# Soft-MoE after attention: the bias and maximum rows of the score matmuls held in bfloat16, with single buffers for two scratch tiles and more weights fetched in attention

## The chip, the cores and the metric

The kernel runs on one NeuronCore of one Trainium2 chip. The metric is the device time of one execution in microseconds (us), as the median of several runs. Beside it stands one profiled execution of the kernel before, whose rows are read below: its own time is 441.82 us and its span (first to last instruction) 440.1 us, so 1.7 us lie around the span.

The engines are TensorE (PE; its weight loads are listed as PEld), VectorE (DVE), ScalarE (ACT), GpSimd (POOL) and SyncE (SP), which here does nothing but issue DMAs.

## The reference

Eight batches of causal attention with eight heads (576 positions, head size 64) and a bias made of running sums, and behind them one soft mixture of experts over all 4608 tokens (8 experts of 4 slots, 512 to 1024 to 512). The inputs q and k are the drawn values times 8. Cut to what is computed:

```python
scores = q @ k.T / 8                                   # per head, 576 x 576
cum    = cumsum(max(s, 0))
bias   = -(cum[:, None] - cum[None, :])
scores = where(causal, -1e9, scores + min(bias, 0))
attn   = exp(scores - max(scores)); attn /= attn.sum() + 1e-9
x      = (attn @ v) as 4608 rows of 512
logits = x @ phi                                       # 32 slots
d      = softmax(logits over the tokens)               # dispatch
h      = relu((d.T @ x)[expert] @ w1[expert]); slot_out = h @ w2[expert]
out    = softmax(logits over the slots) @ slot_out
```

## The kernel before

**The work.** The 64 heads are taken as 32 pairs p, four pairs to a batch; the two heads of a pair use the two halves of TensorE's rows. For each pair the program makes these steps (their names are those of the planner):

- load and load_v bring q, k and v; cast and low split q and k into a high and a low part in a tile w (float32r).
- A tile g carries what is added to the scores through a matmul of its own. Its rows hold ones, the parts of the running sums (step cum, a DMA, L293) and the parts of the row maxima (step md, a DMA, L359). Three such tiles turn over.
- mx (L311) computes approximate scores with the high parts, and adds the sums with a second matmul whose weights are the tile ones2. red (L323) lets DVE add the mask and take the maximum of each row: twelve instructions with accumulator for a pair, each followed by a short read of the accumulator. Their full-size output goes to a scratch tile, junk, and is never read; junk has two buffers.
- f0 (POOL, L338 and L339) splits the maxima in two parts, f1 (PE, L346) transposes them, f2 (ACT) copies them out of PSUM, and md writes them into g.
- s (L377) computes the scores from four matmuls per block: three of w's parts, and the last with g, which adds the bias and takes the maximum away. ex (ACT, L388) takes the exponential, cut (POOL, L395) zeroes what lies above the diagonal.
- zc and z (POOL, L421 to L427) add up the columns, ax and a (PE, L467 and L478; rows named x and y) multiply with v, ev (ACT, L490) copies the result out of PSUM, and sm (L507) sums rows with a tile of unit columns, onesl.

For each batch, e1 (L595) takes the reciprocals of the sums, rw (L600) writes them to DRAM (rows rs<-sr) and rd (L517) reads them back broadcast (rows arena<-rs); nr (L540) multiplies. nat transposes the result, lt (L619, L623) computes the logits, c0 to c1 copy and transpose them, and t2 to t8 keep a running maximum (nmin, L733), running totals (tot) and running slot inputs (acc, L779). For the last pair the reciprocals come through a matmul instead (rb), and nr is L537.

**The combine weights.** Eight more chains, one per batch, turn the softmax over slots into operands for the last stage: sp (L698 on DVE, L700 on ACT, L702 on DVE) writes three parts of a batch's values to a tile en, ct (PE, L709, rows ctb and cta) transposes them, and cd (L717 and L718, DVE for even batches and ACT for odd ones) copies them out of PSUM. ct of any batch waits for all of s. en has two buffers, so sp of batch b waits for ct of batch b-2. Their result is not used before the last stage.

**After attention.** m0 to m7 finish the slot softmax (pt at L824, i4s at L830). sit (L941) scales acc by i4s; mlp1 (L954), relu, mlp2 (L988), pick (L997) and the combining matmul (L1020) follow, and 18 transfers of 512 KB write the output (L1028).

**The weights.** w1 and w2 are fetched as 64 quarters of 512 KB. NPRE of them (21) go to a tile of their own, pre, during attention. As attention's buffers come free another 22 follow: 17 pieces of the arena, the two halves of one w tile (ww), and the three g tiles (wg, through the helper `slot`). The remaining 21 wait until the first quarters have been used.

**What sets the order.** A planner, `schedule` (L34), orders all steps on the five engines by list scheduling: it knows for each step an estimated time, the steps it comes after, and an urgency from the table PR (L21). PE's queue, and each other engine's, then runs in that order whatever the real times are. Where the planner sees PE idle ahead of the first a step or after the last, `busy` matmuls (L914) fill the gap.

## Time and profile before

| | before |
|---|---|
| median of 3 runs | 446.05 us (444.98 to 446.85) |
| profiled execution | 441.82 us |
| its span | 440.1 us |
| mean granted TensorE clock | 0.978 of full speed |
| busy: PE, PEld, DVE, ACT, POOL | 406.3, 302.5, 309.6, 245.4, 281.4 us |
| DMA | 83.21 MB, mean 189 GB/s |

The rows shown below come from views of that one execution. A row of a timeline gives the start in us, the duration in us, the engine, the line of the kernel, the operation, output<-input, its shape and count, and in brackets the idle time of the engine ahead of it with what ended that wait. In the chain of waits a row gives the start, the duration and the work that held up the end at that time. A row of windows gives a stretch, its length, for each engine its busy time and instructions, the granted clock, the busy share of the DMA engines and GB/s.

### The profile page before, as it was taken

To read this page: it belongs to the slowest core of one execution; us is meant where nothing else is said; L and a number is where in the kernel's file an instruction comes from. 1 tells how busy PE (TensorE), PEld (TensorE's weight loads), DVE (VectorE), ACT (ScalarE), POOL (GpSimd) and SP (SyncE) were. 2 spreads that over 40 slices of the span, in tenths; PEclk is the share of its full clock that TensorE was granted. 3 is DMA by queue.
4 is the path that set the end of the run, shared out by engine and by line. 5 is a ranking of instruction groups with operands and counts; after the bars stand their busy time and mean duration, and the time that the engine had idled before them with its cause. 6 is when DMAs were issued, how large, how long until landed. Compare 5 with 4: busy or idle time off the path is not lost.

```text
span 440.1 us, 14686 instructions
## 1 busy us (share of the span) xinstructions
PE 406.3 (92%) x5625; PEld 302.5 (69%) x5625; DVE 309.6 (70%) x1055; ACT 245.4 (56%) x732; POOL 281.4 (64%) x385
## 2 busy tenths in 40 slices
PE   7999999989999999999999999999999999898960
PEld 6787777777677767766877687777776857344550
DVE  6777767987887888779877887788778486121460
ACT  3146676576658665856675676567665745011350
POOL 7349889878877895888588858887887710000000
PEclk9599999999999999999999999999999999999995
DMA  5317565626664475448544822362247389999988
GB/s 175 108 57 236 157 174 155 212 87 189 193 180 131 137 217 157 131 136 225 152 132 136 231 90 84 105 178 82 87 114 216 95 291 337 392 402 409 384 297 293
DMA packets 54549, 83.21 MB, mean 189 GB/s; under 512 B 5456, under 2 KB 41808, under 8 KB 54480
## 3 DMA queue, kind: packets, MB, share of 16 engines
q1 hardware_dynamic: 54480, 82.29, 59.6%
q8 instruction: 44, 0.72, 0.7%
q14 instruction: 25, 0.20, 0.1%
HBM read 71.84 MB, written 10.06 MB: 186 GB/s over the span
## 4 chain that ended last, share of the span: by engine, by line
PE 66%; DMA 12%; DVE 9%; issue 5%; SPq 3%; POOL 2%; ACT 1%; DVEq 0%
PE s L377 19%; PE y L478 15%; PE mx L311 10%; DMA arena<-rs 7%; PE m L954 3%; DMA rs<-sr 3%; PE m L988 3%; PE sum L507 3%; SPq L517 2%; DVE nmin L733 2%; PE busy L914 2%; PE lt L619 2%; PE nat L548 2%; PE po L1020 2%; DVE junk L323 1%
## 5 line engine op out<-in xcount | busy, mean ns | idle before, releaser
L323 DVE CUSTOM_DVE_ANT_0 junk<-mx,mask 128x448 bf16<-128x448 f32 (+3 forms) x320 | 125.5, 427 | 50.8 <-PE mx L311 25.1
L388 ACT ACTIVATE arena<-s 128x288 f32<-128x288 f32 (+4 forms) x384 | 114.3, 409 | 30.0 <-PE s L377 29.3
L377 PE MATMUL s<-w 64*128 64x288 f32 (+4 forms) x1152 | 109.2, 304 | 0.0
L478 PE MATMUL y<-arena 128*64 128x512 f32 (+4 forms) x640 | 90.1, 427 | 0.0
L377 PEld LDWEIGHTS s<-w 64*128 64x128 f32 (+1 forms) x1152 | 81.7, 177 | 10.1 <-ACT arena L388 1.2
L395 POOL TENSOR_SCALAR_AFFINE_SELECT arena<-arena 128x256 f32<-128x256 f32 (+1 forms) x160 | 69.0, 444 | 23.7 <-ACT arena L388 21.7
L478 PEld LDWEIGHTS y<-arena 128*64 128x64 f32 x640 | 43.0, 137 | 46.4 <-issue 35.8
L421 POOL TENSOR_TENSOR arena<-arena 128x896 f32<-128x896 f32 x31 | 66.4, 2141 | 7.5 <-PE mt L346 5.2
L311 PE MATMUL mx<-w 64*128 64x288 f32 (+4 forms) x384 | 59.3, 314 | 3.7 <-DVE e_nat L664 2.7
L311 PE MATMUL mx<-g,ones 64*128 64x288 f32 (+4 forms) x384 | 56.0, 308 | 1.7 <-DVE ones L227 1.7
L377 PE MATMUL s<-g 64*128 64x288 f32 (+4 forms) x384 | 56.5, 291 | 0.0
L423 POOL TENSOR_TENSOR arena<-arena 128x640 f32<-128x640 f32 x31 | 48.0, 1547 | 2.6
L278 ACT CAST w<-arena 128x576 fp32r<-128x576 f32 x64 | 39.8, 675 | 15.0 <-DMA arena<-in_qk_dram 15.0
L283 DVE TENSOR_TENSOR w<-arena,w 128x576 fp32r<-128x576 f32 x64 | 48.0, 776 | 0.0
L311 PEld LDWEIGHTS mx<-w 64*128 64x128 f32 x384 | 41.1, 190 | 8.1 <-PE s L377 3.8
L490 ACT COPY arena<-y 128x512 f32<-128x512 f32 x32 | 18.8, 588 | 47.0 <-PE y L478 47.0
L311 PEld LDWEIGHTS mx<-g,ones 64*128 64x128 f32 x384 | 41.0, 191 | 2.4 <-POOL g L217 1.9
L540 DVE TENSOR_TENSOR arena<-arena 128x576 f32<-128x576 f32 x31 | 34.7, 1128 | 8.7 <-DMA arena<-rs 8.4
L377 PEld LDWEIGHTS s<-g 64*128 64x128 f32 (+1 forms) x384 | 35.1, 177 | 0.7 <-DMA g<-hl 0.2
L338 POOL TENSOR_SCALAR mh<-mx 128x10 fp32r<-128x10 f32 x32 | 21.5, 672 | 20.4 <-DVE mx L323 20.3
L425 POOL TENSOR_TENSOR arena<-arena 128x384 f32<-128x384 f32 x31 | 31.4, 1013 | 2.4
L323 DVE CUSTOM_DVE_ANT_0 junk<-mx,mask,mx 128x288 bf16<-128x288 f32 x64 | 30.6, 516 | 2.2 <-PE mx L311 1.2
(157 smaller groups left out, 565.8 us busy)
## 6 DMA issues: line engine op xcount, KB each, us to landing
pre<-in_w_dram SPq DMA_DIRECT2D x38, 512.0 KB
arena<-in_qk_dram SPq DMA_DIRECT2D x32, 576.0 KB
arena<-in_w_dram SPq DMA_DIRECT2D x18, 512.0 KB
arena<-rs SPq DMA_DIRECT2D x62, 144.0 KB
arena<-in_v_dram SPq DMA_DIRECT2D x32, 256.0 KB
out_dram<-arena SPq DMA_DIRECT2D x11, 512.0 KB
out_dram<-pre SPq DMA_DIRECT2D x7, 512.0 KB
wg<-in_w_dram SPq DMA_DIRECT2D x5, 512.0 KB
```

Source lines behind the costliest of these rows:

```text
L278: nc.scalar.copy(w[:, QO + S * i:QO + S * (i + 1)], st["raw", p][:, i, :])
L283: nc.vector.tensor_tensor(w[:, QO + S * (2 + i):QO + S * (3 + i)], st["raw", p][:, i, :], w[:, QO + S * i:QO + S * (i + 1)].bitcast(F32), ...
L311: nc.tensor.matmul(ps[a][:, d:d + hi - lo], l[r], t[r, KO + lo:KO + hi], start=t is w, stop=t is gt)
L323: nc.vector.tensor_tensor_reduce(out=junk[r, 0:w], in0=ps[r, d:d + w], in1=mask[r, o:o + w], scale=1.0, scalar=m[:, a, 4:5] if i == 1 else ...
L377: nc.tensor.matmul(ps[a][0:n, d:d + hi - lo], t[r, ko + 128 * j:ko + 128 * j + n], t[r, qo + lo:qo + hi], start=x == 0, stop=x == 3)
L388: nc.scalar.activation(st["p", p][0:n, a, o + lo:o + hi], ps[0:n, d:d + hi - lo], AF.Exp, bias=0.0, scale=0.125)
L395: nc.gpsimd.affine_select(d, d, pattern=[[0, 2], [1, n]], compare_op=ALU.is_ge, fill=0.0, base=0, channel_multiplier=-1)
L421: eng.tensor_tensor(z[:, :, 128:576], pt[:, :, 128:576], pt[:, :, 576:1024], op=ALU.add)
L423: eng.tensor_tensor(z[:, :, 256:576], z[:, :, 256:576], pt[:, :, 1024:1344], op=ALU.add)
L425: eng.tensor_tensor(z[:, :, 384:576], z[:, :, 384:576], pt[:, :, 1344:1536], op=ALU.add)
L478: nc.tensor.matmul(y[r, lo - 64:512], vt[:, j, r], st["p", p][:, g, OFF[j] + lo - 128 * j:OFF[j] + 576 - 128 * j], start=(j == 0), stop=(j ...
L540: nc.vector.tensor_tensor(u, u, st.pop(("r", p)), op=ALU.mult)
```

## The change

- The running sums are split into three bfloat16 parts (before: two of float32r), the maxima into two bfloat16 parts. The tiles g, ones2, mask, mh and hl are bfloat16, so the second matmul of mx, the last of s, and the transpose f1 have bfloat16 operands; f1 uses a bfloat16 identity, identb, made at the start.
- onesl is one window of 63 columns instead of 16 tiles of 32; ph is held once instead of four times over.
- junk has one buffer instead of two, and en has one, so sp of batch b waits for ct of batch b-1.
- The g tiles no longer become weight slots. NPRE is 25, so 25 quarters go to pre, 19 to freed room, and 20 wait.
- The table of urgencies PR stays as it is.

The diff, cut to its core:

```diff
-NPRE = 21
+NPRE = 25
...
-    cumhl = reg("x", 0)[0:NH, 0:2 * S].rearrange("p (l x) -> p l x", l=2)
-    nc.vector.tensor_copy(cumhl[:, 0, :].bitcast(F32R), cum)
-    nc.vector.tensor_tensor(cumhl[:, 1, :].bitcast(F32R), cum, cumhl[:, 0, :], op=ALU.subtract)
-    cumd = pd.tile([NH, 2, S], F32, tag="cum", name="cumd", bufs=1)
+    cumhl = reg("x", 0)[0:NH, 0:3 * S // 2].bitcast(BF16).rearrange("p (l x) -> p l x", l=3)
+    for l in range(3):
+        nc.vector.tensor_copy(cumhl[:, l, :], cum)
+        if l < 2:
+            nc.vector.tensor_tensor(cum, cum, cumhl[:, l, :], op=ALU.subtract)
+    cumd = pd.tile([NH, 3, S], BF16, tag="cum", name="cumd", bufs=1)
...
-    onesl = one.tile([128, 4 * HP, 32], F32, name="onesl")
+    onesl = one.tile([128, 63], F32, name="onesl")
     nc.vector.memset(onesl, 0.0)
-    for a in range(4 * HP):
-        nc.vector.memset(onesl[:, a, a:a + 1], 1.0)
+    nc.vector.memset(onesl[:, 31:32], 1.0)
...
-    ph = one.tile([128, HP, 4 * NS], F32, name="ph")
+    ph = one.tile([128, HP, NS], F32, name="ph")
...
-        t = slot("g", [128, PAD + 2 * S], F32R, f"g{i}")
+        t = one.tile([128, PAD + 2 * S], BF16, name=f"g{i}")
...
-            mask = one.tile([128, S], F32, name="mask")
+            mask = one.tile([128, S], BF16, name="mask")
...
-        (nc.vector if i else nc.gpsimd).memset(t.bitcast(F32), 0.0)
+        (nc.vector if i else nc.gpsimd).memset(t, 0.0)
         for a in (0, 64):
-            nc.gpsimd.memset(t[a:a + 4, 0:KO].bitcast(F32), 1.0)
-            nc.gpsimd.memset(t[a:a + 4, KO:].bitcast(F32), -1.0)
+            nc.gpsimd.memset(t[a:a + 5, 0:KO], 1.0)
+            nc.gpsimd.memset(t[a:a + 5, KO:], -1.0)
...
-    ones2 = one.tile([128, 128], F32R, name="ones2")
+    ones2 = one.tile([128, 128], BF16, name="ones2")
...
+    identb = one.tile([128, 128], BF16, name="identb")
+    nc.vector.tensor_copy(identb, ident)
...
-                junk = p2.tile([128, 448], BF16, tag="junk", name="junk")
+                junk = p2.tile([128, 448], BF16, tag="junk", name="junk", bufs=1)
...
-            mh = p2.tile([128, 2, 2, NCH], F32R, tag="mh", name=f"mh{p}")
+            mh = p2.tile([128, 2, 2, NCH], BF16, tag="mh", name=f"mh{p}")
...
-            nc.tensor.transpose(ps[0:4 * NCH, 0:128], mh.rearrange("p a l c -> p (a l c)").bitcast(F32), ident)
+            nc.tensor.transpose(st["mt", p], mh.rearrange("p a l c -> p (a l c)"), identb)
...
-            hl = p2.tile([4 * NCH, 128], F32R, tag="hl", name=f"hl{p}")
+            hl = p2.tile([4 * NCH, 128], BF16, tag="hl", name=f"hl{p}")
...
-                nc.tensor.matmul(st["lt", b][32 * g:32 * g + 32, 64:192], ph[:, hp, 32 * g:32 * g + 32],
+                nc.tensor.matmul(st["lt", b][32 * g:32 * g + 32, 64:192], ph[:, hp, :],
...
-                st["en", b] = p2.tile([128, NCH, 3, NS], F32R, tag="en", name=f"en{b}")
+                st["en", b] = p2.tile([128, NCH, 3, NS], F32R, tag="en", name=f"en{b}", bufs=1)
...
-        war = [("ct", b - 2)] if b > 1 else []
+        war = [("ct", b - 1)] if b else []
...
-    for kind, n in (("g", NG), ("w", NW)):
+    for kind, n in (("w", NW),):
```

Three places show how instructions move. A row gives the line, the operation, output<-input and the shape. Lines after about L190 are two to four higher in the kernel after.

On DVE, at the program's start, the kernel before splits the sums (arena rows after the scan), sets constants and clears two g tiles:

```order
L179 SCALAR_TENSOR_TENSOR arena<-arena 64x576
L182 CAST arena<-arena 64x576
L183 TENSOR_TENSOR arena<-arena 64x576
L189 MEMSET onesl 128x512
L191 MEMSET onesl 128x1 x16
L194 MEMSET dn 64x128
L214 MEMSET g_134 128x1216
L214 MEMSET g_145 128x1216
L225 MEMSET ones_157 128x128
```

The kernel after, at the same place on DVE:

```order
L179 SCALAR_TENSOR_TENSOR arena<-arena 64x576
L183 CAST arena<-arena 64x576
L185 TENSOR_TENSOR arena<-arena 64x576
L183 CAST arena<-arena 64x576
L185 TENSOR_TENSOR arena<-arena 64x576
L183 CAST arena<-arena 64x576
L192 MEMSET onesl 128x63
L193 MEMSET onesl 128x1
L196 MEMSET dn 64x128
L216 MEMSET g_122 128x608
L216 MEMSET g_133 128x608
L227 MEMSET ones_145 128x64
```

Three instructions on 64x576 have come in ahead of the memsets; the memsets of onesl have become two small ones, and those of g have half the elements.

On SP, in the last pairs of the last batch, the kernel before issues weight quarters (in_w) between the reciprocals' way out (rs<-sr) and back (arena<-rs); rs_0 carries the first two pairs, rs_1 pair 30:

```order
L517 DMA arena<-rs_0_6801 64x2x288 x4
L836 DMA wg_6921<-in_w_dram 128x1024
L836 DMA ww_6932<-in_w_dram 128x1024
L600 DMA rs_1_6947<-sr_6934 128x72
L836 DMA arena<-in_w_dram 128x1024 x3
L517 DMA arena<-rs_1_6947 64x2x288 x2
L836 DMA ww_6932<-in_w_dram 128x1024
```

The kernel after, at the same place on SP:

```order
L521 DMA arena<-rs_0_6787 64x2x288 x4
L840 DMA ww_6907<-in_w_dram 128x1024
L604 DMA rs_1_6931<-sr_6918 128x72
L840 DMA ww_6907<-in_w_dram 128x1024
L521 DMA arena<-rs_1_6931 64x2x288 x2
L840 DMA arena<-in_w_dram 128x1024 x15
```

One quarter instead of two stands ahead of rs<-sr, and one instead of three between it and its way back. The four more quarters of pre stand earlier on SP, in pairs 25 to 28.

On PE, between the end of attention and the first matmul of the experts, the kernel before runs as follows (the figure behind a name is the batch; sl is t7, ctb and cta are ct):

```order
L709 MATMUL ctb6_7218<-ident_61,en6_7186 96x128
L709 MATMUL cta6_7217<-ident_61,en6_7186 96x128 x4
L805 MATMUL pn_7226<-one1_74,mrow_7211 128x1
L771 MATMUL sl7_7229<-arena_77,dn_120 32x512 x4
L775 MATMUL sl7_7229<-arena_77,dn_120 32x128 x4
L709 MATMUL ctb7_7244<-ident_61,en7_7224 96x128
L709 MATMUL cta7_7243<-ident_61,en7_7224 96x128 x4
L824 MATMUL pt_7258<-tot_72,cst_sb_60 128x1
L941 MATMUL sit_7278<-i4s_67,acc_68 128x32 x4
```

The kernel after, at the same place on PE:

```order
L713 MATMUL ctb5_7218<-ident_61,en5_7204 96x128
L713 MATMUL cta5_7217<-ident_61,en5_7204 96x128 x4
L828 MATMUL pt_7226<-tot_72,cst_sb_60 128x1
L916 MATMUL busy_7237<-ident_61 128x128 x3
L713 MATMUL ctb6_7242<-ident_61,en6_7230 96x128
L713 MATMUL cta6_7241<-ident_61,en6_7230 96x128 x4
L916 MATMUL busy_7254<-ident_61 128x128 x5
L713 MATMUL ctb7_7261<-ident_61,en7_7250 96x128
L713 MATMUL cta7_7260<-ident_61,en7_7250 96x128 x4
L943 MATMUL sit_7283<-i4s_67,acc_68 128x32 x4
```

The transposes of batches 6 and 7, which stood ahead of pt, now stand between pt and sit, with eight busy matmuls.

On DVE at the same place, the kernel before finishes the parts of en and the copies of ct ahead of acc and tot:

```order
L702 TENSOR_TENSOR en_7224<-e_nat,en_7224 128x5x32
L717 CAST ct_6978<-cta_7217 96x512
L718 CAST ct_6978<-ctb_7218 96x64
L810 COPY fac<-pn 128x1
L779 SCALAR_TENSOR_TENSOR acc<-acc,al_7171,sl_7229 128x512
L819 SCALAR_TENSOR_TENSOR tot<-tot 128x1
L820 TENSOR_TENSOR tot<-tot,fac 128x1
L828 TENSOR_SCALAR tot<-pt 128x1
L829 RECIPROCAL tot<-tot 128x1
L830 TENSOR_SCALAR i4s<-cst_sb,tot,fac 128x32
L943 COPY sit<-sit 128x128
```

The kernel after, on DVE from tot to sit:

```order
L824 TENSOR_TENSOR tot<-tot,fac 128x1
L702 CAST en_7230<-e_nat 128x5x32
L832 TENSOR_SCALAR tot<-pt 128x1
L833 RECIPROCAL tot<-tot 128x1
L834 TENSOR_SCALAR i4s<-cst_sb,tot,fac 128x32
L706 TENSOR_TENSOR en_7230<-e_nat,en_7230 128x5x32
L721 CAST ct_6962<-cta_7241 96x512
L722 CAST ct_6962<-ctb_7242 96x64
L702 CAST en_7250<-e_nat 128x5x32
L706 TENSOR_TENSOR en_7250<-e_nat,en_7250 128x5x32
L945 COPY sit<-sit 128x128
```

The last part of batch 6's en, the copies of its ct and both parts of batch 7's en on DVE have moved behind i4s; between acc and tot there are now the copies of batch 4's ct and parts of batch 5's en.

More of the change, by code (lines that the diff above doesn't have):

```diff
@@ L155, in slot @@
     def slot(kind, shape, dtype, name):
-        return keep.tile(shape, dtype, tag=kind, name=name, bufs=dict(g=NG, w=NW)[kind])
+        return keep.tile(shape, dtype, tag=kind, name=name, bufs=NW)
     def reg(kind, i):
@@ L223, in tile_attn_softmoe @@
         ws.append(t)
-    ones2 = one.tile([128, 128], F32R, name="ones2")
-    nc.vector.memset(ones2.bitcast(F32), 0.0)
+    ones2 = one.tile([128, 128], BF16, name="ones2")
+    nc.vector.memset(ones2, 0.0)
     for a in (0, 64):
-        nc.vector.memset(ones2[a:a + 2].bitcast(F32), 1.0)
+        nc.vector.memset(ones2[a:a + 3], 1.0)
+    identb = one.tile([128, 128], BF16, name="identb")
+    nc.vector.tensor_copy(identb, ident)
     mx = []
@@ L292, in cum @@
             for a in range(2):
-                nc.sync.dma_start(out=gt[64 * a:64 * a + 2, KO:KO + S].bitcast(F32),
+                nc.sync.dma_start(out=gt[64 * a:64 * a + 3, KO:KO + S],
                                   in_=(cumhl if p < HP else cumd)[2 * p + a:2 * p + a + 1, :, :])
@@ L336, in f0 @@
             use("mx", p, 3)
-            mh = p2.tile([128, 2, 2, NCH], F32R, tag="mh", name=f"mh{p}")
+            mh = p2.tile([128, 2, 2, NCH], BF16, tag="mh", name=f"mh{p}")
             nc.gpsimd.tensor_scalar(mh[:, :, 0, :], m, 1.0, None, op0=ALU.mult)
-            nc.gpsimd.tensor_tensor(mh[:, :, 1, :], m, mh[:, :, 0, :].bitcast(F32), op=ALU.subtract)
+            nc.gpsimd.tensor_tensor(mh[:, :, 1, :], m, mh[:, :, 0, :], op=ALU.subtract)
             st["mh", p] = mh
@@ L345, in f1 @@
             ps = bank("mt")
-            nc.tensor.transpose(ps[0:4 * NCH, 0:128], mh.rearrange("p a l c -> p (a l c)").bitcast(F32), ident)
-            st["mt", p] = ps
+            st["mt", p] = ps[0:4 * NCH, 0:64].bitcast(BF16)
+            nc.tensor.transpose(st["mt", p], mh.rearrange("p a l c -> p (a l c)"), identb)
         op(("f1", p), "PE", 110, (t0, "f1"), f1, [("f0", p), dep("md", old(2))], bank=1, ldw=17)
         def f2():
-            hl = p2.tile([4 * NCH, 128], F32R, tag="hl", name=f"hl{p}")
-            nc.scalar.copy(hl, st.pop(("mt", p))[0:4 * NCH, 0:128])
+            hl = p2.tile([4 * NCH, 128], BF16, tag="hl", name=f"hl{p}")
+            nc.scalar.copy(hl, st.pop(("mt", p)))
             st["hl", p] = hl
@@ L358, in md @@
             for a in range(2):
-                nc.sync.dma_start(out=gt[64 * a + 2:64 * a + 4, 0:KO].bitcast(F32).rearrange("l (c q) -> l c q", c=NCH),
-                                  in_=hl[2 * NCH * a:2 * NCH * (a + 1)].bitcast(F32))
+                nc.sync.dma_start(out=gt[64 * a + 3:64 * a + 5, 0:KO].rearrange("l (c q) -> l c q", c=NCH),
+                                  in_=hl[2 * NCH * a:2 * NCH * (a + 1)])
         op(("md", p), "SP", 1300, (t0, "md"), md, [("f2", p)], dma=28)
@@ L506, in sm @@
                         c = S // 2 * f + SQ * i
-                        nc.tensor.matmul(y[o:o + 32, 0:SQ], onesl[:, 4 * hp + i, :], st["z", p][:, g, c:c + SQ],
+                        nc.tensor.matmul(y[o:o + 32, 0:SQ], onesl[:, 31 - 4 * hp - i:63 - 4 * hp - i], st["z", p][:, g, c:c + SQ],
                                          start=first and i == 0, stop=final and i == 3)
@@ L618, in lt @@
             for g in range(4):
-                nc.tensor.matmul(st["lt", b][32 * g:32 * g + 32, 64:192], ph[:, hp, 32 * g:32 * g + 32],
+                nc.tensor.matmul(st["lt", b][32 * g:32 * g + 32, 64:192], ph[:, hp, :],
                                  st["u", p][:, 64 + 128 * g:192 + 128 * g], start=hp == 0, stop=hp == HP - 1)
             for g in range(4):
-                nc.tensor.matmul(st["lt", b][32 * g:32 * g + 32, 0:64], ph[:, hp, 32 * g:32 * g + 32],
+                nc.tensor.matmul(st["lt", b][32 * g:32 * g + 32, 0:64], ph[:, hp, :],
                                  st["u", p][:, 0:64], start=False, stop=hp == HP - 1, skip_group_check=True)
@@ L888, in get @@
                 dst = arena[:, F * i:F * (i + 1)]
-            elif kind == "g":
-                dst = slot("g", [128, F], F32, f"wg{i}")
             else:
@@ L1090, in layout @@
     HP = H // 2
-    phi = np.tile(moe_phi.reshape(HP, 128, -1).transpose(1, 0, 2), (1, 1, 4))
+    phi = moe_phi.reshape(HP, 128, -1).transpose(1, 0, 2)
     arrays = dict(qk=qk, v=vn, s=s.reshape(B * H, S), phi=phi, w1=w1, w2=w2, cst=constants())
```

## The prediction, made before the kernel was run

> **What bounds the kernel now.** I read the page's busy shares first, then the chain of waits, then windows over its stages, and last the timelines at the places that the change touches. The page:
>
> ```profile
> PE 406.3 (92%) x5625; PEld 302.5 (69%) x5625; DVE 309.6 (70%) x1055; ACT 245.4 (56%) x732; POOL 281.4 (64%) x385
> PE 66%; DMA 12%; DVE 9%; issue 5%; SPq 3%; POOL 2%; ACT 1%; DVEq 0%
> ```
>
> PE is busy for 92% of the span, and the chain that ended last runs over PE for 66% of it. Two rows of the chain, the first transpose of nat in two batches, and the windows of a stretch in attention and of the stages behind it:
>
> ```profile
> 207.11 0.66 PE nat L548 x4
> 250.30 0.66 PE nat L548 x4
> ...
> 250.00:330.00 80.00, 78.63 (x1163) 59.88 (x1165) 63.55 (x230) 51.54 (x159) 64.59 (x84) 1.00 0.39 108
> 380.00:400.00 20.00, 19.39 (x216) 8.20 (x212) 3.10 (x5) 2.39 (x4) 0.00 (x0) 1.00 1.02 396
> 400.00:422.00 22.00, 19.13 (x224) 10.46 (x216) 7.10 (x12) 6.66 (x13) 0.00 (x0) 1.00 1.03 385
> 422.00:426.00 4.00, 3.64 (x30) 3.65 (x31) 3.40 (x7) 2.86 (x6) 0.00 (x0) 1.00 0.63 220
> ```
>
> A batch takes 250.30 - 207.11 = 43.19 us, and in 250 to 330 PE is busy for 78.63 of 80 us: attention goes at PE's pace, and another engine counts only where PE waits for it. From 380 to 422 the DMA engines are full (396 and 385 GB/s) and PE is nearly so (19.39 of 20 us). From 422 to 426, before the last outputs, DMA falls to 0.63 of its time and 220 GB/s: the last outputs wait for PE's results, not for the queue of weights. So four fewer weight quarters behind attention (2.1 MB, 5.3 us at 396 GB/s) are worth nothing by themselves at the end; I price them there at 0.
>
> **The change part by part.** The sum is made against the profiled execution, 441.82 us (span 440.1 and 1.7 around it). The median of the runs, 446.05, is 4.2 us above it, so I add the sum to the median.
>
> *Startup.* DVE, POOL and PE before the first maxima:
>
> ```profile
> 5.48 0.66 DVE L182 CAST arena<-arena 64x576 fp32r<-64x576 f32 x1
> 6.18 0.75 DVE L183 TENSOR_TENSOR arena<-arena 64x576 fp32r<-64x576 f32 x1
> 6.98 0.48 DVE L189 MEMSET onesl<- 128x512 f32 x1
> 8.29 1.07 DVE L214 MEMSET g<- 128x1216 f32 x1 [0.30 <-issue]
> ...
> 9.42 0.62 POOL L216 MEMSET g<- 4x640 f32 x1 [1.76 <-DVE g L214]
> ...
> 14.41 0.42 PE L311 MATMUL mx<-w 64*128 64x64 f32 x2 [0.83 <-POOL w L222]
> ```
>
> A cast takes one slot of 0.70 us (5.48 to 6.18), a subtraction one of 0.80 (to 6.98). Two casts and one subtraction more are +2.2 us. The memset of onesl (0.48) and its sixteen small ones (about 0.2) nearly go: -0.7. If the g memsets cost by elements, two times half of 1.07 go: -1.1; making identb is put at 0.2. DVE comes out +0.6, and POOL, which waits 1.76 us for DVE's memset of g at 9.42 and holds PE until 14.41, starts about 1.1 later. POOL's eight strips at 0.62 behind that could cost as much as now, or half in bfloat16 (-2.4). With DVE's extra waits of the next part in this stage, where PE has no store of work, I take +0.8 us, between -1.3 (POOL's half-price strips) and +2.0.
>
> *DVE's waits for junk.* With one junk buffer a maximum instruction must wait for the one in front. A steady pair on DVE, and POOL's step behind it:
>
> ```profile
> 56.13 0.46 DVE L323 CUSTOM_DVE_ANT_0 junk<-mx,mask 128x288 bf16<-128x288 f32 x1 [1.39 <-POOL arena L395]
> 56.52 0.08 DVE L323 DVE_READ_ACCUMULATOR2_ANT mx<- 128x1 f32 x1
> 56.52 0.45 DVE L323 CUSTOM_DVE_ANT_0 junk<-mx,mask 128x288 bf16<-128x288 f32 x1
> ...
> 58.16 0.49 DVE L323 CUSTOM_DVE_ANT_0 junk<-mx,mask 128x320 bf16<-128x320 f32 x1 [1.18 <-PE mx L311]
> ...
> 60.09 0.08 DVE L323 DVE_READ_ACCUMULATOR2_ANT mx<- 128x1 f32 x1
> 60.20 0.23 DVE L323 CUSTOM_DVE_ANT_0 junk<-mx,mask 64x64 bf16<-64x64 f32 x1
> ...
> 62.46 0.69 POOL L338 TENSOR_SCALAR mh<-mx 128x10 fp32r<-128x10 f32 x1 [0.22 <-DVE mx L323]
> ...
> 81.16 0.62 DVE junk L323
> ...
> L548 PE MATMUL nat<-ident,arena 128*128 128x128 f32 x128 | 18.6, 276 | 5.6 <-DVE mx L323 5.6
> ```
>
> Now one such instruction starts with the accumulator read of the one before (both 56.52). Where it can't overlap, it starts 0.11 us later (read at 60.09, next at 60.20). Six of a pair's twelve overlap today, so the price is 6 x 0.11 = 0.66 us of DVE in a pair. DVE idles 1.39 and 1.18 us in a pair (56.13, 58.16), which takes it in; but five of the six lie behind the second gap, so the last maxima come up to 0.55 us later, and POOL's mh starts straight after them. The chain goes over DVE's maxima at 81.16, in the second batch, where I count 0.4 for PE; and PE's nat, whose idle time in front (5.6 us over the eight batches) ends with a maximum of DVE, I count as 0.11 later in each of seven batches, 0.8. I take +1.2 us for both. If the slack takes everything it is 0; if none is taken, 32 x 0.66 = 21 us, which is a rival. The Trainium skill, "VectorE: DVE Perf Modes", section "The DRAIN you can't avoid", says that a semaphore between chained DVE operations costs nothing extra. By that this term would be 0 and the time 449.95. The rows 56.52 and 60.20 speak against it for this instruction, since the overlap is there to be lost.
>
> *bfloat16 in PE.* Steps of the two heads of a pair:
>
> ```profile
> 62.33 0.30 PE L377 MATMUL s<-g 64*128 64x288 f32 x2
> 62.46 0.47 PE L377 MATMUL s<-w 64*128 64x192 f32 x6
> 62.77 0.28 PE L377 MATMUL s<-g 64*128 64x192 f32 x2
> 62.88 0.80 PE L377 MATMUL s<-w 64*128 64x448 f32 x6
> ```
>
> A step over 288 columns (two matmuls, one in each half of the rows) lasts 0.13 us (62.33 to 62.46); one over 192 lasts 0.11 (62.77 to 62.88) where 0.13 x 192 / 288 would be 0.087. So a short step is held at 0.11, by its weights of 128 columns, it seems. Each pair has three such steps on the changed operands: 192 columns in s, 192 and 64 in mx. If bfloat16 loads its weights in the same time, the change is 0, which I take, since the trace has no such load. If in half the time, 0.024 + 0.024 + 0.055 = 0.10 us for a pair, 3.3 us in all.
>
> *Earlier weights.* The four extra quarters fall in pairs 25 to 28, where the window 250 to 330 shows DMA 0.39 busy: 0, at most +1 where they meet a read-back. Mask, mh, hl, the half-sized DMAs of g and the smaller phi lie on engines and queues with idle time: 0; were their cover gone, they are tenths of a microsecond.
>
> *The tail.* The last reciprocals' way, and what waits for it:
>
> ```profile
> 354.05 6.96 DMA rs<-sr
> 361.70 4.36 DMA arena<-rs
> ...
> 366.75 0.81 DVE L537 TENSOR_TENSOR arena<-arena,rb 128x288 f32<-128x288 f32 x2
> 366.89 0.43 PE L619 MATMUL lt<-arena,ph 128*32 128x128 f32 x8 [0.75 <-DVE arena L540]
> ...
> 364.74 0.58 ACT L490 COPY arena<-y 128x512 f32<-128x512 f32 x1 [3.41 <-PE y L478]
> ```
>
> rs<-sr takes 6.96 us, behind two quarters, and the read-back 4.36 behind three. With one quarter each they would land some 3 us sooner (three quarters of 0.52 MB less at 396 GB/s are 4 us). But then the last pair binds: its copy on ACT ends at 365.32 and its scaling on DVE starts at 366.75, so 1.35 us are won. I take -1.4. Against it stands the order of the combine weights:
>
> ```profile
> 372.11 0.29 PE L709 MATMUL ctb<-ident,en 128*96 128x128 f32 x1
> 372.23 0.60 PE L709 MATMUL cta<-ident,en 128*96 128x128 f32 x4
> ...
> 372.40 0.32 DVE L698 CAST en<-e_nat 128x160 fp32r<-128x160 f32 x1
> 372.75 0.32 DVE L702 TENSOR_TENSOR en<-e_nat,en 128x160 fp32r<-128x160 f32 x1
> 372.99 0.68 DVE L717 CAST ct<-cta 96x512 fp32r<-96x512 f32 x1
> 373.59 0.21 DVE L718 CAST ct<-ctb 96x64 fp32r<-96x64 f32 x1
> 376.46 0.30 DVE L830 TENSOR_SCALAR i4s<-cst_sb,tot,fac 128x32 f32<-128x32 f32 x1
> ...
> 376.91 1.05 PE L941 MATMUL sit<-i4s,acc 128*128 128x32 f32 x8 [0.88 <-DVE i4s L830]
> ```
>
> A ct takes PE 0.72 us (372.11 to 372.83), DVE picks it up after 0.16 (372.99), its copies take 0.81 (to 373.80), a cast of en 0.33, the subtraction 0.33, and PE starts 0.15 after that. Behind i4s, where today 0.15 us pass before sit (376.76 to 376.91), there now stand in this order: the subtraction for batch 6 (0.30), handover and ct (0.87), pick-up and copies (0.97), cast and subtraction for batch 7 (0.67), handover and enough of ct (0.65). That is 3.46 against 0.15, so +3.3. Ahead of i4s the copies of batch 4, en of batch 5 and its ct before pt add, over what idle time takes in, 1.2. With one en buffer these links can't be drawn together. The tail gives -1.4 + 1.2 + 3.3 = +3.1 us, between -0.5 (the ct hidden to one link) and +4.5. From sit on PE has little room to catch up (the windows from 380 on), so I let it go through to the end.
>
> The sum: 0.8 + 1.2 + 0 + 0 + 3.1 = +5.1 us, 446.9 for a profiled execution, 451.15 for the median, rounded: **451 us**.
>
> **The rivals.**
>
> *PE's bfloat16 steps are faster.* For it: 0.11 against 0.087 above. Against it: the trace has no bfloat16 matmul. The three short steps give -3.3 us, so 447.85, within 0.5%, 443.8 to 448.3 (about what a measurement of this kernel can tell from no change). The Trainium skill, "TensorE: Matmul & The Clock Gate", section "Weight-path perf modes — Fast Weight Load (FWL) and DoubleRow", says that a load of 128 weights is fast when the type is not FP32, about twice as fast measured; by that it would be this 447.85. No row here shows it.
>
> *The same, but every changed step gains: faster than before.* A pair has twelve steps on g (six in mx, six in s). If each also lost 0.01 us for the change of weights, and the 64-column one all but its columns (0.13 x 64 / 288 = 0.03 of 0.11), a pair gains 0.12 + 0.024 + 0.024 + 0.08 = 0.25 and 32 pairs 8.0: 443.15 us. It decides from (5.1 + 2.2) / 32 = 0.23 us a pair on.
>
> *Nothing of the tail or of DVE shows.* The links hide behind PE's other work and junk costs nothing; the rs chain stays: 0.8 - 1.4 = -0.6, so 445.45, no change. Against it: i4s to sit is 0.15 us today, with nothing that could hide a link.
>
> *DVE becomes the bound.* If the late maxima go through mh, the transpose and md into s in each pair, up to 0.66 us a pair, half of it is 10.5 us in place of the 1.2: 460.4. Against it: DVE's two gaps, 2.57 us a pair.
>
> **How the numbers follow.** My forecast of 451, with 448.3 to 453.5 as its own bounds: 0.50. PE's short steps: 0.19. All PE steps: 0.11. Nothing shows: 0.12. DVE the bound: 0.08. Faster by over 0.5% is all of the second PE case, and a fifth of the two no-change cases, where startup also falls to its lower bound (0.06): 0.17. Within 0.5% is the rest of these two, 0.25. Slower: 0.50 and 0.08, 0.58. The range leaves out DVE as the bound and most of the second PE case: 443.5 to 456, the upper end from the upper bounds of startup and tail (+1.2, +1.4) and three times the 1.2 that I take for DVE's waits (+2.4).
>
> **What would show it.** Right: in the timeline of DVE, each maximum 0.11 us behind the start of the read in front, the batch still near 43.3 us from nat to nat; on PE sit about 3 us behind its place now, counted from the last sums, with two ct between i4s and sit; rs<-sr nearer to 5 us than 6.96; steps of s on g at 0.13 and 0.11 us. Wrong: a batch shorter by over 0.3 us, which would be PE's bfloat16 steps; or longer by over 1 us, DVE; or sit straight behind i4s.

## The result and the profile after

The kernel after takes 464.68 us (median of 4 runs, 464.19 to 466.1) against 445.51 for the kernel before: a ratio of 1.048 (95% interval 1.043 to 1.053), 19 us slower. Medians here and below are of all runs, while ratios and their intervals leave out runs that lie more than 1.5% above the fastest of the same kernel, so a ratio need not be the quotient of the medians. The prediction was 451 us, with 456 as its upper end. Slower was right; the size was not. The profiled execution took 464.5 us with a span of 462.8, 22.7 more than before. Four marks on PE tell where these lie. The first score matmul starts at 26.65 us (before 26.60). From there to the last group of sums, attention takes 352.15 us instead of 332.93: +19.2. From these sums to sit it is 20.85 instead of 17.37: +3.5. From sit to the end 63.1 instead of 63.2. So nearly everything was lost in attention, where I had put +1.2.

The page of the kernel after, with the busy times and the chain by engine:

```profile
PE 423.0 (91%) x5653; PEld 295.2 (64%) x5653; DVE 325.9 (70%) x1044; ACT 248.4 (54%) x732; POOL 278.5 (60%) x385
PE 65%; DVE 11%; DMA 10%; issue 5%; ACT 2%; POOL 2%; SPq 2%; DVEq 0%
```

PE is "busy" for 16.7 us more at nearly the same work (28 more matmuls of 5625), and DVE's part of the chain has gone from 9% to 11%. The chain's rows for the first nat that stands on it in each batch:

```profile
128.71 0.66 PE nat L552 x4
173.70 0.66 PE nat L552 x4
216.98 0.66 PE nat L552 x4
262.14 0.82 PE nat L552 x4
309.28 0.66 PE nat L552 x4
354.28 0.66 PE nat L552 x4
```

One batch takes 43.28 us (173.70 to 216.98), nearly as the 43.19 us of before that the prediction read; the others take 44.99, 45.16, 47.14 and 45.00. So some batches lose 2 to 4 us in steps. But an even loss lies beneath them, since 43.28 and 43.19 aren't alike: PE idles 1.05 us ahead of the nat that ends the batch of 43.19, and 0.09 ahead of the one that ends the batch of 43.28. The kernel before has one batch without that gap, up to this nat:

```profile
292.40 0.66 PE L548 MATMUL nat<-ident,arena 128*128 128x128 f32 x4
```

From the nat at 250.30 that batch takes 42.10 us, so like for like, without the 0.09, a batch has become 1.1 us longer. Windows of both kernels, from the first score matmul to the nat of the second batch and from there over five batches, first two of the kernel before, then two of the kernel after (the figure behind the length is PE's busy time):

```profile
26.60:120.73 94.13, 91.28 (x1319) 70.53 (x1318) 73.80 (x266) 63.23 (x193) 82.37 (x109) 1.00 0.58 170
120.73:335.60 214.87, 207.99 (x3101) 159.22 (x3101) 172.67 (x598) 140.14 (x429) 173.05 (x226) 1.00 0.51 145
...
26.65:128.71 102.06, 94.63 (x1319) 66.88 (x1318) 82.26 (x269) 64.06 (x193) 82.96 (x109) 0.98 0.53 158
128.71:354.28 225.57, 218.35 (x3101) 154.97 (x3101) 178.65 (x595) 141.87 (x428) 168.72 (x224) 0.98 0.50 145
```

Of the 19.2 us, 7.9 are lost ahead of the nat of the second batch, where PE idles 7.43 us instead of 2.85, mostly behind maxima of DVE, and 10.7 in the five batches behind it, where PE idles hardly longer than before (7.22 us against 6.88). A steady pair on DVE, in the same place as before:

```profile
57.27 0.08 DVE L327 DVE_READ_ACCUMULATOR2_ANT mx<- 128x1 f32 x1
57.49 0.46 DVE L327 CUSTOM_DVE_ANT_0 junk<-mx,mask 128x288 bf16<-128x288 f32 x1
...
59.15 0.08 DVE L327 DVE_READ_ACCUMULATOR2_ANT mx<- 128x1 f32 x1
59.27 0.36 DVE L327 CUSTOM_DVE_ANT_0 junk<-mx,mask 128x192 bf16<-128x192 f32 x1
```

A maximum that waits for the one in front starts 0.12 us after the start of that one's accumulator read (59.15 to 59.27) where DVE is all it waits for, and 0.22 (57.27 to 57.49) where it awaits a matmul of PE too, as most do. From the start of the first maximum (56.88) to the end of the last read (64.11) a pair has 6.46 us of maxima, without its idle 0.77; before it was 5.06 (56.13 to 62.37, less 1.18). That is 1.4 us a pair, twice my 0.66.

### The profile page after: what moved, and what is told of

The parts are those of the page before. It is cut to its first block, busy times and chain, and to the rows that moved or that the text cites. A ratio compares the mean times of both kernels' runs of the same rounds, so it can differ in the third digit from the quotient of the medians.

```text
span 462.8 us, 14711 instructions
## 1 busy us (share of the span) xinstructions
PE 423.0 (91%) x5653; PEld 295.2 (64%) x5653; DVE 325.9 (70%) x1044; ACT 248.4 (54%) x732; POOL 278.5 (60%) x385
## 4 chain that ended last, share of the span: by engine, by line
PE 65%; DVE 11%; DMA 10%; issue 5%; ACT 2%; POOL 2%; SPq 2%; DVEq 0%
PE s L381 20%; PE y L482 16%; PE mx L315 9%; DMA arena<-rs 6%; PE m L990 3%; DVE junk L327 3%; PE m L956 3%; PE sum L511 3%; DVE nmin L737 2%; DMA rs<-sr 2%; PE po L1022 2%; DMA arena<-in_w_dram 2%; PE nat L552 2%; PE lt L623 2%; PE busy L916 1%
## 5 line engine op out<-in xcount | busy, mean ns | idle before, releaser
L327 DVE CUSTOM_DVE_ANT_0 junk<-mx,mask 128x448 bf16<-128x448 f32 (+3 forms) x320 | 137.4, 429 | 52.3 <-PE mx L315 16.4
L381 PE MATMUL s<-w 64*128 64x288 f32 (+4 forms) x1152 | 117.6, 323 | 0.9 <-DVE mx L327 0.9
L482 PE MATMUL y<-arena 128*64 128x512 f32 (+4 forms) x640 | 96.7, 449 | 0.2 <-POOL arena L399 0.2
L381 PEld LDWEIGHTS s<-w 64*128 64x128 f32 (+1 forms) x1152 | 89.3, 178 | 10.7 <-issue 3.3
L315 PE MATMUL mx<-w 64*128 64x288 f32 (+4 forms) x384 | 64.0, 391 | 6.5 <-DVE e_nat L668 2.8
L381 PE MATMUL s<-g 64*128 64x288 bf16 (+4 forms) x384 | 59.3, 286 | 0.0
L315 PE MATMUL mx<-g,ones 64*128 64x288 bf16 (+4 forms) x384 | 53.8, 287 | 1.9 <-DVE ones L229 1.4
L342 POOL TENSOR_SCALAR mh<-mx 128x10 bf16<-128x10 f32 x32 | 20.8, 651 | 52.7 <-DVE mx L327 52.7
L327 DVE DVE_READ_ACCUMULATOR2_ANT mx<- 128x1 f32 (+1 forms) x384 | 31.6, 82 | 0.0
L381 PEld LDWEIGHTS <-g 64*128 64x128 bf16 (+1 forms) x384 | 21.7, 94 | 13.4 <-issue 2.5
```

What stands on the lines that cost most here:

```text
L315: nc.tensor.matmul(ps[a][:, d:d + hi - lo], l[r], t[r, KO + lo:KO + hi], start=t is w, stop=t is gt)
L327: nc.vector.tensor_tensor_reduce(out=junk[r, 0:w], in0=ps[r, d:d + w], in1=mask[r, o:o + w], scale=1.0, scalar=m[:, a, 4:5] if i == 1 else ...
L381: nc.tensor.matmul(ps[a][0:n, d:d + hi - lo], t[r, ko + 128 * j:ko + 128 * j + n], t[r, qo + lo:qo + hi], start=x == 0, stop=x == 3)
L482: nc.tensor.matmul(y[r, lo - 64:512], vt[:, j, r], st["p", p][:, g, OFF[j] + lo - 128 * j:OFF[j] + 576 - 128 * j], start=(j == 0), stop=(j ...
```

## The experiments

All are compared with the kernel before run on the same chip beside them; its medians there were 443.1 to 443.8 us.

**Undoing the single buffers.** With 25 early quarters there is no room in SBUF for second buffers of junk and en, so these runs have 24, and a control has that alone. A fourth puts one junk buffer into the kernel before.

```diff
-NPRE = 25
+NPRE = 24
...
-junk = p2.tile([128, 448], BF16, tag="junk", name="junk", bufs=1)
+junk = p2.tile([128, 448], BF16, tag="junk", name="junk")
...
-st["en", b] = p2.tile([128, NCH, 3, NS], F32R, tag="en", name=f"en{b}", bufs=1)
+st["en", b] = p2.tile([128, NCH, 3, NS], F32R, tag="en", name=f"en{b}")
...
-war = [("ct", b - 1)] if b else []
+war = [("ct", b - 2)] if b > 1 else []
```

The control n24 (the first change of these alone):

> The kernel after with 24 instead of 25 early weight quarters, as the control for the two runs beside it, which need the 4 KB. All theories but one: 464 to 466 us, as the kernel after. If a quarter more in the DMA queues at the batch ends were what makes the attention slow, 461 or less, since one of the batches that lose 3 us would be free of it.

462.14 us, ratio 1.041 (1.034 to 1.049): 0.7% under the kernel after, between the two forecasts, and the two intervals overlap. So what the last early quarter costs stays open, and junk and en are priced against this control.

n24_junk2 (NPRE and junk; its queue on PE is row for row that of the control):

> As the control, with two junk buffers again; PE's order is the same. Theory DVE (single junk costs DVE 1.4 us a pair and throws the scaling of the second pair of a batch against GpSimd's 2.1 us addition; 14 of the 19 us lost in attention): 450 to 452 us, pairs 0.1 to 0.15 us longer than before, no batch of more than 44 us. Rival PE (the bfloat16 matmuls between float32r ones slow TensorE, all 19 us): 463 to 466. Rival DMA (the extra early weights): 463 to 466.

453.64 us, 1.024 (1.017 to 1.030). Junk alone is worth 8.5 us. The time is 1.6 us above the forecast range, and from the second batch's nat on no batch takes over 43.62 us, as forecast. A pair, here and below from its first matmul of s to the next pair's, ahead of the first nat, takes 8.97 us as before, where the control and the kernel after have 9.12.

n24_both2 (all of the diff):

> As the control, with two buffers for junk and for en. Theory DVE plus the order of the combine weights (two transposes behind i4s and the wait of sit for their PSUM bank, about 4 us): 446 to 448.5 us, sit within 0.5 us of i4s. Rival PE: 460 to 463 (the tail alone comes back). If the tail's order costs nothing: as the run beside it.

450.13 us, 1.015 (1.010 to 1.020): en is worth 3.5 us, and sit again starts 0.15 us behind i4s. But 1.5% stay, more than the theory left.

bef_junk1 (the kernel before with `bufs=1` for junk):

> The kernel before with one junk buffer, and nothing else. Theory DVE: 456 to 461 us, with the maxima on DVE 0.11 to 0.23 us apart and batches of 45 to 47 us where the second scaling meets GpSimd. Rival PE: 445 to 447, as before. A price of 0.66 us of DVE a pair that is all taken in by idle time: 446 to 447.

456.14 us, 1.028 (1.023 to 1.034). The single junk buffer costs the kernel before 12 us, with no bfloat16 matmul anywhere. Its pairs take 9.11 us. The time is as forecast, but where it lies is mostly not. The first nat of each batch on the chain, from the second on:

```profile
127.86 0.66 PE nat L548 x4
171.50 0.66 PE nat L548 x4
214.47 0.66 PE nat L548 x4
257.77 0.66 PE nat L548 x4
302.89 0.66 PE nat L548 x4
345.85 0.66 PE nat L548 x4
```

Of these five batches the fourth, which has the only blocked scaling (3.02 us), takes 45.12 us, the others 43.0 to 43.6. Together the five lose 3.1 us on the kernel before. From the first score matmul (26.96) to the nat at 127.86 it loses 6.8, and from the last sums to sit 3.4.

**Why a few DVE waits cost that much.** The scaling of a batch's second pair (nr) on DVE, in the batch of 47.14 us and in the one of 43.28 us of the kernel after, with GpSimd beside the first:

```profile
305.24 3.18 DVE L544 TENSOR_TENSOR arena<-arena 128x576 f32<-128x576 f32 x1
...
214.61 0.75 DVE L544 TENSOR_TENSOR arena<-arena 128x576 f32<-128x576 f32 x1
...
303.49 1.89 POOL L399 TENSOR_SCALAR_AFFINE_SELECT arena<-arena 128x256 f32<-128x256 f32 x4
305.35 2.10 POOL L425 TENSOR_TENSOR arena<-arena 128x896 f32<-128x896 f32 x1
307.40 0.40 POOL L399 TENSOR_SCALAR_AFFINE_SELECT arena<-arena 128x256 f32<-128x256 f32 x1
...
309.28 0.66 PE L552 MATMUL nat<-ident,arena 128*128 128x128 f32 x4 [1.97 <-DVE mx L327]
```

The same instruction takes 3.18 us or 0.75. In the slow case it starts 0.2 us later (9.97 us after the end of e1, at 295.27, instead of 9.78, after 204.83), because its reciprocals land later (its start waits for the DMA arena<-rs, which the fast one doesn't). GpSimd's selections end then, its addition of 2.10 us begins at 305.35, and the scaling ends only once that and the selection behind it are through. The next maxima wait, and PE idles 1.97 us ahead of nat. In the two profiles of the kernel after (the second below), from the second batch on, seven scalings that started by 9.78 us took 0.75 us, and all five from 9.87 on took 2.8 to 3.3. (In bef_junk1 the five at 9.96 took 0.75 us and the one at 10.39 took 3.02, so the moment is another in another kernel.) Such a blocked scaling is not new: in the kernel before, five of the six from the second batch on take 1.9 to 2.7 us. New is the length of PE's gap behind it, 1.97 us where it was 1.05. The Trainium skill, "SBUF — State Buffer", section "SBUF: two separate sides", describes a lock on a shared port, which a DVE instruction with two inputs in SBUF or a GpSimd instruction holds to its end; the trace agrees that DVE stands still, for 2.4 us more than the 0.75 that its work takes. Then comes the clock. The windows of the kernel after behind that gap, with the granted clock third from the end:

```profile
309.30:310.30 1.00, 1.00 (x6) 0.60 (x8) 0.87 (x4) 0.32 (x1) 0.92 (x2) 0.99 0.77 179
310.30:313.30 3.00, 3.00 (x12) 0.99 (x10) 2.38 (x11) 0.26 (x1) 1.03 (x2) 0.50 0.33 93
313.30:314.30 1.00, 1.00 (x12) 0.66 (x8) 1.00 (x4) 0.00 (x0) 0.50 (x1) 0.80 0.03 8
```

For 3.4 us PE runs at 0.50 of its clock, which costs 1.71 us (the batch with such a fall and no gap takes 44.99 us, the one without either 43.28); the kernel before shows this nowhere in attention, with gaps of up to 1.30 us. The kernel after shows it four times, 6.8 us. In all profiles, 13 of 17 PE gaps over 1.8 us in attention were followed by such a fall, 6 of the 29 between 1.17 and 1.7 us, and none of those up to 1.11 us.

So of the 19.2 us the falls make 6.8 and longer idle time 4.9, nearly all of it ahead of the second batch's nat. Another 5.2 are the even loss of the five batches, about 1.05 in each.

Three runs were to test the part of the scaling and the clock. The first two cut GpSimd's addition into one instruction for each head:

```diff
-                eng.tensor_tensor(z[:, :, 128:576], pt[:, :, 128:576], pt[:, :, 576:1024], op=ALU.add)
+                for a in range(2):
+                    eng.tensor_tensor(z[:, a, 128:576], pt[:, a, 128:576], pt[:, a, 576:1024], op=ALU.add)
```

In the kernel after (aft_zsplit):

> The kernel after with GpSimd's 2.1 us addition (zs, first step) as two instructions, one for each head. Theory of the shared resource (DVE's scaling of the batch's second pair waits for the GpSimd instruction that runs, 2.8 to 3.2 us instead of 0.75, PE then idles 1.98 us and its granted clock falls to a half for 3.4 us): the scaling takes at most 2 us in any batch, PE's gap ahead of nat is under 1.2 us, no or one drop of the clock in attention instead of four, 455 to 460 us. Rival (the single junk buffer delays the maxima by itself, the scaling only happens to be long): 463 to 466, gaps of 2 us stay.

459.56 us, 1.037 (1.030 to 1.045), but not as I had it: three blocked scalings still take 3.1 to 3.5 us, with gaps of 2.1 us and three falls of the clock in attention. That the time lies in the forecast range is luck. In the kernel before (bef_zsplit):

> The same split in the kernel before, where the scaling takes 2.0 to 2.7 us and PE idles 1.05 us ahead of nat in five batches, with no fall of the clock. Theory of the shared resource: the scaling takes 1.0 to 1.7 us, the gap falls under 0.4 us, 441 to 444 us against 445, or 4 us less in the profile's attention. Rival: no change, or 1 us slower by the extra instructions on GpSimd.

446.97 us, 1.008 (1.005 to 1.011): 0.8% slower, against both forecasts. Its scalings take 2.3 to 3.3 us, longer than uncut. So DVE doesn't get in between two GpSimd additions that follow each other, and the idea that one instruction's length is what DVE waits for falls; in this the runs differ from the lock of the Trainium skill, as cited above. That DVE and GpSimd exclude each other here stays as the reading that fits the rows.

The third puts fillers ahead of that nat, in the kernel after (aft_fill):

```diff
+            if hp == 1 and b < B - 1:
+                for i in range(4):
+                    nc.tensor.matmul(ps[:, 0:128], ident, ident, start=True, stop=True)
```

> The kernel after with four filler matmuls on PE (1.1 us, into the PSUM bank of nat, no reader) ahead of the nat of a batch's second pair, so that PE's wait of 1.98 us for the scaling is broken up. Theory of the clock: a PE gap above some 1.1 us lets the granted clock fall to a half for 3.4 us, 1.7 us each; with the fillers the gap is 0.9 us, no fall ahead of any nat, and where the scaling is not blocked they cost up to 1.1 us: 461 to 464 us, and batches with a blocked scaling 1.7 us shorter (45.3 instead of 47.1). Rival, the half clock has another cause (the load of DMA or GpSimd at that place): the falls stay, 465 to 468.

466.53 us (459.4 to 468.7), 1.047 (1.035 to 1.059): inconclusive. In its profile no scaling of these was blocked, so there was no gap to fill; the clock never fell in attention. So it doesn't test the clock, but it shows what is left without blocked scalings and falls: attention takes 345.99 us there, with seven groups of fillers of some 0.94 each (a batch takes 44.22 instead of 43.28). Without these it is, by estimate, 339.4, still 6.5 us more than the 332.93 of the kernel before.

A second profile of the kernel after (aft_again):

> The kernel after once more, one profile. Theory of the race: GpSimd or DVE gets the second scaling by where the reciprocals land (DVE if it can start by 9.78 us after e1, else a block to 12.9 or later), so the batches that lose 2.8 to 3.9 us may be others than before, while pairs inside a batch again take 9.12 us and sit comes 4.2 us behind i4s. If the same four falls of the clock at the same batches show, it is no race but the order.

462.62 us. Two scalings are blocked, at two of the three batches where the first profile has one; at the third, where it took 2.95 us, it takes 0.75 here. The clock falls three times in attention, at the places of three of the first profile's four falls, and sit again stands 4.19 us behind i4s. So how many batches lose differs from one execution to the next, as in a race, but not freely: none of them is a new one.

**The order of the combine weights.** bef_en1 is the kernel before with one en buffer and `war = [("ct", b - 1)] if b else []`:

> The kernel before with one en buffer and sp of batch b waiting for ct of batch b-1; nothing else. Theory of the tail's order (after i4s two transposes, their copies, and the wait of sit for the PSUM bank of the last copy: 4.2 us in the kernel after against 0.15 before): 3 to 5 us slower than before, all of it between the last sums and sit. Rival, the links hide: within 1 us of before.

445.71 us, 1.006 (1.002 to 1.009), so 1.9 to 2.6 us, less than the 3 to 5 of the forecast. In its profile the way from the last sums to sit is 4.4 us longer, but only 1.88 us stand between i4s and sit, and attention is 0.9 shorter, with three scalings that weren't blocked. The tail of the kernel after (ACT's row is the copy of batch 7):

```profile
395.15 0.30 DVE L834 TENSOR_SCALAR i4s<-cst_sb,tot,fac 128x32 f32<-128x32 f32 x1
395.82 0.29 PE L713 MATMUL ctb<-ident,en 128*96 128x128 f32 x1 [0.44 <-DVE en L706]
398.14 0.29 PE L713 MATMUL ctb<-ident,en 128*96 128x128 f32 x1 [0.47 <-DVE en L706]
399.38 0.21 ACT L722 CAST ct<-ctb 96x64 fp32r<-96x64 f32 x1
399.64 1.08 PE L943 MATMUL sit<-i4s,acc 128*128 128x32 f32 x8 [0.78 <-ACT ct L722]
```

Two transposes stand behind i4s as forecast, and sit waits for a third thing that I had left out: the copy of batch 7, which ends at 399.59. From i4s to sit it is 4.19 us. The reciprocals' way gave some back: from e1 of pair 30 to its nr it is 11.1 us (372.25 to 383.34), where before 12.9 passed (353.15 to 366.08).

**What is left: the bfloat16 matmuls.** n21_both2 is n24_both2 with 21 early quarters:

> The kernel after with two buffers for junk and en and with 21 early quarters as in the kernel before: what is left of the change are the bfloat16 rows, the smaller constants and three slots fewer behind attention. Theory of the bfloat16 rows (some 0.4 us at each batch end and one or two drops of the clock stay): 447 to 450 us. Rival, the early weights make what was left: 443 to 446, as before.

452.64 us, 1.023 (1.016 to 1.030), above both forecasts. So the early weights are not what was left; whether they help isn't shown, since the interval overlaps that of n24_both2. Then the order of the four matmuls of a block of s was turned round, so that the bfloat16 one comes first:

```diff
-enumerate(((w, KO, QO), (w, KO + 2 * S, QO), (w, KO, QO + 2 * S), (gt, KO, QO))):
+enumerate(((gt, KO, QO), (w, KO, QO), (w, KO + 2 * S, QO), (w, KO, QO + 2 * S))):
```

n24_gfirst is n24_both2 with that:

> As n24_both2, but in s the bfloat16 matmul of a block comes first instead of last of the four. If the change between bfloat16 and float32r on TensorE has a price at each switch, it stays: 449 to 451 us. If the price lies in the one place where the bfloat16 64x64 block is followed by a 128-column float32r load (0.15 against 0.06 us of step), that moves to the front of the block: s of a pair 0.1 us shorter, 446 to 449. In both cases pairs inside a batch are near 8.97 us.

440.19 us, 0.994 (0.991 to 0.998): 10 us less, far under both forecasts, and 0.6% under the kernel before. Pairs take 8.72 us, where both forecasts had 8.97. Rows of a pair's s on PE, from the first block to the sums behind it, of the kernel before:

```profile
61.83 0.66 PE L377 MATMUL s<-w 64*128 64x288 f32 x6
...
62.88 0.80 PE L377 MATMUL s<-w 64*128 64x448 f32 x6
...
63.93 0.65 PE L377 MATMUL s<-w 64*128 64x288 f32 x6
...
64.54 0.29 PE L311 MATMUL mx<-w 64*128 64x288 f32 x2
...
64.90 0.33 PE L507 MATMUL sum<-arena,onesl 128*32 128x72 f32 x7
```

The same of n24_both2, bfloat16 last, whose blocks start with float32r as before:

```profile
280.80 0.66 PE L381 MATMUL s<-w 64*128 64x288 f32 x6
...
281.79 0.84 PE L381 MATMUL s<-w 64*128 64x448 f32 x6
...
283.06 0.67 PE L381 MATMUL s<-w 64*128 64x288 f32 x6
...
283.60 0.39 PE L315 MATMUL mx<-w 64*128 64x288 f32 x2
...
284.06 0.46 PE L511 MATMUL sum<-arena,onesl 128*32 128x72 f32 x16
```

And of n24_gfirst, whose blocks start with the bfloat16 matmul:

```profile
52.94 0.30 PE L381 MATMUL s<-g 64*128 64x288 bf16 x2
...
53.91 0.36 PE L381 MATMUL s<-g 64*128 64x448 bf16 x2
...
55.15 0.30 PE L381 MATMUL s<-g 64*128 64x288 bf16 x2
...
55.69 0.29 PE L315 MATMUL mx<-w 64*128 64x288 f32 x2
...
56.05 0.71 PE L511 MATMUL sum<-arena,onesl 128*32 128x72 f32 x32
```

The differences of starts in a fence are the times of four pieces. Blocks of 288 and 192 columns: 1.05 us before, 0.99 and 0.97 with bfloat16. Blocks of 448 and 64: 1.05, then 1.27 and 1.24. The second block of 288: 0.61, 0.54 and 0.54. mx: 0.36, 0.46 and 0.36. In n24_both2 mx's float32r matmul stands behind a bfloat16 one, and that costs the 0.10. In sum s and mx lose 0.19 us with the bfloat16 matmul last and 0.04 with it first. From the sums to y, where the transpose f1 and the rest of mx stand, the two gain 0.20 and 0.31 (3.05 us before from the chain's sum at 47.03 to y at 50.08, then 2.85 and 2.74). So bfloat16 is faster on PE, by about a quarter of a microsecond a pair in n24_gfirst; in n24_both2 its place in s takes just that away.

The three last runs. aft_gfirst is the kernel after with this order alone:

> The kernel after with the bfloat16 matmul first of the four in s, and nothing else; one buffer for junk and en as it has them. Theory: the place of the bfloat16 step in the 64x64 block costs PE 0.26 us a pair (8.3 us in all), by itself, and the single buffers cost the rest: 452 to 458 us, pairs of 8.7 to 9.0 us, batches with a blocked scaling and sit 4.2 us behind i4s as in the kernel after. If the single junk buffer keeps DVE as the one that sets the pace, it comes to 461 to 465. If the order of the four alone was behind the loss: 442 to 446.

459.3 us, 1.034 (1.025 to 1.044), pairs of 8.84 us: 5.4 us less, 1.3 above the first forecast, and the losses of the single buffers stay. bef_gfirst is the kernel before with it:

> The kernel before with the same order of the four matmuls, all of float32r. Theory, it is the bfloat16 type in that place: no change, 442 to 445 us, pairs of 8.97 us. If any last row of four in the 64x64 block has the price: 435 to 440.

444.16 us, 1.000 (0.997 to 1.004), pairs of 8.96: float32r doesn't care. n24_gmxfirst is n24_gfirst with the same in mx:

```diff
-for l, t in ((w[:, q0 - 128:q0], w), (ones2, gt)):
+for l, t in ((ones2, gt), (w[:, q0 - 128:q0], w)):
```

> As n24_gfirst, with the bfloat16 matmul first in mx too. If a bfloat16 step followed by a float32r one of 128 columns is where time is lost, nothing changes in mx, since the two alternate either way: 438 to 442 us. If being last in the accumulation costs: another 0.1 us a pair, 435 to 438.

437.77 us, 0.986 (0.982 to 0.990), pairs of 8.68: the fastest of all, 1.4% under the kernel before. The pairs gained 0.04 us, between nothing and the 0.1 of the two forecasts, so the run doesn't settle which holds. It is the kernel after with second buffers for junk and en, one early quarter less, and the bfloat16 matmuls first.

## Why the prediction was wrong

The step that failed is the one on junk: "I take +1.2 us for both", with all the rest of DVE's waits left to its idle time, "which takes it in". The runs put 8.5 us (of n24) to 12 us (of the kernel before) on junk. The step was wrong in three ways.

- **The price of a wait.** I took 0.11 us from a row where an instruction waits for DVE alone. Most maxima wait for PE as well, and those take 0.22 (57.27 to 57.49). A pair costs DVE 1.4 us, not 0.66, and the rule cited there, by which the wait would cost nothing, doesn't hold for these instructions. The idle time doesn't take it all in: a pair takes 9.11 us in bef_junk1 and 9.12 in n24 against 8.97 in the kernel before and in n24_junk2. If each of 32 pairs loses these 0.14 to 0.15 us, they are, by estimate, 4.5 to 4.8 us.
- **What the delay meets.** I looked for PE's rows behind a late maximum and found 0.11 us a batch. The delay in fact lengthens PE's gaps where PE waits for a maximum: behind a blocked scaling from 1.05 to 1.97 us, and ahead of the second batch's nat from 2.85 to 7.43 us in all. The rows were there before: nr took 0.76 to 2.7 us in one and the same kernel, and I didn't ask why.
- **What a longer gap does to the clock.** 1.05 us of PE idle cost 1.05 us before. 1.97 us cost 1.97 and, mostly, 1.71 more at half clock. I had the clock as a constant. The Trainium skill, "TensorE: Matmul & The Clock Gate", section "Part 1: The HAM clock gate (the "warmup" mystery)", has two states, half and full clock, and a window of some 3.4 us that runs freely. The trace agrees with these (0.50, and 1.71 us lost, which is 3.4 us at half), and a free window would explain why one gap of 2 us is followed by a fall and another isn't. The Trainium skill has the fall come after an idle window of that length; here gaps of 1.2 to 2.3 us were enough. I had read none of it against the gaps.

The rival "DVE becomes the bound", at 460 us, was the nearest to the result in time. Its mechanism holds in part: a delay does reach the pairs, but with 0.15 us each and not 0.33, and gaps and the clock make most of the rest. The prediction's own sign for DVE, a batch longer by over 1 us, is what came.

A second step failed, bfloat16 in PE at 0. From the kernel before to n24 it is 18.3 us: junk 8.5, en 3.5, and 6.3 by which n24_both2 still lies above the kernel before. With the bfloat16 matmul first in s these 6.3 turn into a gain of 3.1, so the place of that matmul, which the prediction didn't ask about, is worth 9 to 10 us.

The other steps, in the prediction's order:

- **Startup**, +0.8: the first score matmul comes 0.05 us later. In other executions it lies between 25.8 and 27.5 us whatever the kernel, so there was nothing to see.
- **bfloat16 in PE**, 0: right for a pair ahead of the first nat, by luck, and wrong for the kernel. n24_both2 has pairs of 8.97 us like the kernel before, but as the balance of a gain and a loss of some 0.2 us each, and its batches are longer: 43.58 us with a gap of 0.89, where the kernel before has 43.19 with 1.05. That is half of the even loss of the kernel after. The rival with 0.25 us a pair had the gain's size; it came out only when the order of the matmuls was changed. The loads of g take 93 ns instead of 185 (rows below, of the kernel before and of n24_both2), which agrees with the "about twice as fast" that the prediction cited from the Trainium skill, "TensorE: Matmul & The Clock Gate", section "Weight-path perf modes — Fast Weight Load (FWL) and DoubleRow". The blocks of 288 and 192 columns are 0.06 us shorter. For the rival I had 0.024 there; the loss at the 448- and 64-column blocks, 0.22, I had not expected at all.

```profile
L377 PEld LDWEIGHTS s<-g 64*128 64x128 f32 x320 | 30.6, 185 | 0.7 <-DMA g<-hl 0.2
...
L381 PEld LDWEIGHTS <-g 64*128 64x128 bf16 x320 | 15.7, 93 | 14.6 <-issue 6.5
```

- **Earlier weights**, 0: no loss is shown up to 24 quarters, since n21_both2 is no faster than n24_both2. The clock doesn't tell them apart: between the first score matmul and the output stage both profiles have 6.8 us at half clock, n21_both2 all of it behind sit, n24_both2 half of it in attention. The step from 24 to 25 stays open.
- **The tail**, +3.1: +3.5 in the profile. The terms were -1.4 for the reciprocals (about -1.8 measured), +1.2 ahead of i4s (from that nr to i4s 11.81 us instead of 10.38, so +1.4), and +3.3 behind i4s (4.19 against 0.15, so +4.0, with the wait for the last copy that I had missed). n24_junk2 against n24_both2 gives 3.5 us.

What stays open: why the 448- and 64-column blocks are slower with bfloat16, in either order; whether fillers would save the clock, since the run for it met no gap; how junk's price divides between the pairs, the gaps and the clock, since the profiles differ in it from one execution to the next; and why n24_both2 loses at its batches' ends what n24_gfirst doesn't.

## What to carry to other kernels

Taking a second buffer away from a scratch tile that nobody reads can cost more than its space buys (here 8.5 to 12 us): look at every instruction that writes it, and price the wait at the row of an instruction that waits for as many engines. When two batches seem equal, compare their gaps too, since a shorter gap can hide a longer batch. Where an engine shares something with another, a delay of a tenth of a microsecond can decide who goes first, so look for rows of one instruction with two very different durations before calling a delay covered. When operands change type, try the order of the matmuls in an accumulation as well: here it was worth 2%.

## What the runs showed of the hardware that was not expected

- PE's granted clock falls to 0.50 for 3.4 us after gaps far shorter than that: after 13 of 17 gaps of 1.8 to 2.3 us, after 6 of 29 of 1.17 to 1.7, and after none up to 1.11.
- A DVE instruction with two inputs in SBUF waits for more than one GpSimd addition: 3.22 us in aft_zsplit, where GpSimd's two halves took 2.23 together.
- A wait for a second engine adds 0.11 us to the start of a DVE instruction (0.22 against 0.11).
- A bfloat16 matmul among three float32r ones can cost more by its place in the accumulation than its faster load saves: 450.13 us with it last, 440.19 with it first. With float32r alone the order did nothing (ratio 1.000).
